# An attention and feed-forward kernel: the first product as seven block products of batch pairs

## The chip, the core and the metric

The kernel runs on one core of a Trainium2 chip. A core has TensorE (PE) for matmuls, with its weight loads shown apart as PEld; VectorE (DVE), ScalarE (ACT) and GpSimd (POOL) for element-wise work; and SyncE (SP), which here issues every DMA. The metric is the device time of one execution in microseconds.

## The reference, cut to what matters

```python
q, k, v: (8, 12, 448, 64)          # batch, heads, sequence, head size
q_n, k_n = rmsnorm(q, g_q), rmsnorm(k, g_k)
scores = matmul(q_n, k_n^T) / 8
attn = softmax(scores)             # with the maximum taken off, sum + 1e-9
x = matmul(attn, v)                # brought to (8 * 448, 768)
h = x @ w_in                       # (3584, 768) @ (768, 2048)
g = h * cos(h)
out = g @ w_out                    # (3584, 2048) @ (2048, 768)
```

w_in and w_out come as float64. Inside the kernel they are decoded from their integer halves into float32.

## The kernel before

Two heads of one batch form a pair; 48 pairs (u), six to a batch, run one after the other. Work on a pair: square sums and norms of q and k; seven score tiles S (`score`); their row minima on DVE (`rowmin`; the scores are negated) and exponentials P on ACT (`expo`); then per chunk of keys (kc, four of them) seven transposes of P into the tile PT (`transp`), copies of PT to SBUF (`pt_high`, `pt_low`), and the product P v into O. The sums' reciprocals take a way through DRAM (`rs_copy`, `rs_store`, `rs_load`) and scale O to x, with features in the partitions.

There are two ways to multiply here. Plain float32 operands go into one matmul, which the trace records as two. Split operands are a high part in fp32r (tile names with `hi`) and a low part, the rest (`lo`); three fp32r matmuls, hi hi, hi lo and lo hi, then make one product. Pairs in `S32` have plain scores, pairs in `A32` plain P v; before, both are the pairs 0 to 8. In a pair of `A32` P v is `av_whole` (L522): per chunk one matmul for each of the two heads, side by side in the halves of O. In the others it is `av` (L514): seven fp32r matmuls for each head with split P and split v, for which ACT makes `hi` (L494), DVE `lo` (L502, L504), POOL splits v (L409, L413), and x is put together from two halves (L540, L545, L548).

The first product, h = x w_in, runs per batch b as soon as its six pairs are there: 16 column blocks fc of w_in, each 18 matmuls (6 chunks of features by 3 parts, L573 to L575) into a bank `ph`, copied on ACT (`h_out`, L585) and stored to the DRAM tensor `h_d`. All split columns of w_in stay in SBUF. The first product of a batch is mixed into the attention of the next batch; that of the last batch stands alone behind the attention.

The second product, out = g w_out, already works on pairs of batches with seven block products in place of eight (the scheme of Strassen and Winograd, halving features, rows and batches): seven forms of w_out, made while attention runs and kept in the DRAM tensor `wo_d`, are streamed in through SBUF slots (`v_place`), 7 x 8 x 9 matmuls of each of three banks for a batch pair (L648 to L650).

What sets the order is the class `Plan`. Every piece of work is added with an engine, a cost, a due time, the keys it reads and writes, and for DMAs a landing time. `Plan.order` simulates the engines with these costs, takes on a free engine the ready piece that is due first, and so fixes each engine's order, which then stands in the program. Buffers are rings (`RING`): a piece waits for the user that many instances earlier. There is one plan for attention and the mixed first product and one for the rest. The pace of the pairs in the first plan is set by `base(u)`.

Of the kernel before, what the change touches and what calls it, by code (L numbers as in the profile page):

```python
# [3 lines left out]

# [23 lines left out]
class Plan:  # L28
# [40 lines left out]
    def order(self):  # L69
        parts = self.parts  # L70
        for (name, inst), users in self.users.items():
            parts[users[0]][5].update(self.users.get((name, inst - self.rings[name]), ()))
            parts[users[0]][5].update(self.users.get((name, inst - 1), ())[:1])
# [17 lines left out]
        while True:  # L91
# [21 lines left out]
            for m in after[n]:  # L113
                same = parts[m][0] == e and not land
# [12 lines left out]
def tile_attention_moe(  # L127
# [19 lines left out]
    S32, A32 = tuple(range(9)), tuple(range(9))  # L147
# [12 lines left out]
    epool = ctx.enter_context(tc.tile_pool(name="epool", bufs=2))  # L160
# [11 lines left out]
    wo_d = dpool.tile([NH, NPR, 128, 2, HM], F32, tag="wo_d", name="wo_d")  # L172
# [16 lines left out]
    def g_fold():  # L189
# [5 lines left out]
    wts, wfl, raw = {}, {}, {}  # L195
    RING = {
        "sd": 1, "r": 5, "rkb": 1, "rqb": 1, "kd": 1, "kl": 2, "khi": 2, "qd": 1, "ql": 2, "qhi": 2, "vd": 1, "vs": 2, "S": 3, "sm": 3, "P": 12,
        "hi": 4, "lo": 2, "O": 1, "xf": 6, "rs": 1, "rt": 1, "ph": 1, "he": 2, "wf": 2,
        "wx": 5, "wv": 2,
    }  # L200

    def w_load(fc):
        if f64:
            st = raw[fc] = wpool.tile([128, 2 * DM], I32, tag=f"w{fc}", name=f"raw{fc}")
            nc.sync.dma_start(st, w_in[fc].bitcast(I32))
        else:
            wfl[fc] = apool.tile([128, DM], F32, tag="wf", name=f"wf{fc}", bufs=RING["wf"])
            nc.sync.dma_start(wfl[fc], w_in[fc])
# [38 lines left out]
    def v_fetch(k, m):  # L247
        fc, cs = k + NH * (m // 2), slice(m % 2 * HM, m % 2 * HM + HM)
        f = mix[(k, m)] = apool.tile([128, HM], F32, tag="wx", name=f"wx{k}_{m}", bufs=RING["wx"])
        if f64:  # L250
            st = half[(k, m)] = apool.tile([128, DM], I32, tag="wf", name=f"rawo{k}_{m}", bufs=RING["wf"])
            nc.sync.dma_start(st, w_out[fc][:, cs].bitcast(I32))
        else:
            nc.sync.dma_start(f, w_out[fc][:, cs])

    def v_decode(k, m, step):
        decode(half[(k, m)], mix[(k, m)], step)

    def v_mix(k, to, a, c, op):
        if to == SS and (k, SS) not in mix:  # L260
            mix[(k, SS)] = apool.tile([128, HM], F32, tag="wx", name=f"wx{k}_{SS}", bufs=RING["wx"])
        nc.gpsimd.tensor_tensor(mix[(k, to)], mix[(k, a)], mix[(k, c)], op)
# [3 lines left out]
    def v_split(k, p, m, lo):  # L266
        if not lo:
            t = vts[(k, p)] = apool.tile([128, 2, HM], F32R, tag="wv", name=f"wv{k}_{p}", bufs=RING["wv"])
            nc.scalar.copy(t[:, 0, :], mix[(k, m)])
# [4 lines left out]
    def v_store(k, p):  # L274
        nc.sync.dma_start(wo_d[k, ORDER.index(p)], vts.pop((k, p)).bitcast(F32))
# [787 lines left out]
```

## Time and profile before

| | us |
|---|---|
| median of 3 runs | 1442.18 (1441.9 to 1447.97) |
| the profiled execution, as run | 1444.56 |
| its span, first to last instruction | 1442.7 |
| batch 0's first product begins | 89 |
| pair 12 done with x | 231.2 |
| attention's last x | 953.7 |
| last batch's first product alone | 959.5 to 1017.7 |
| second product and end | 1017.7 to 1442.7 |

The times within the execution are from the start of its span. The page lists for every engine its busy time; the groups list instructions of one line and shape with their mean duration; the windows give per stretch each engine's busy time and, in brackets with an x, how many instructions began there. PE's durations overlap from one matmul to the next, so counts per stretch tell more of PE than busy time.

### The profile page before, as it was taken

Reading aid. Unit: us, or ns where it says so; the run is one execution under the profiler, and the core shown is the slowest. Engines: PE = TensorE matmul, PEld = TensorE weight load, DVE = VectorE, ACT = ScalarE, POOL = GpSimd, SP = SyncE. Lnnn points to the kernel's source line nnn. Section 1 sums busy time; section 2 is a strip of 40 time slices with the busy share of each in tenths; the row PEclk is TensorE's granted clock in tenths of the full one; section 3 lists DMA queues with packets and bytes.
Section 4 is the critical chain, followed back from the end, with each engine's and each line's share of the span. In section 5 each row is a group of like instructions: output and inputs, shape, how many; then the busy total and the mean of one; then the engine's idle time right before and its main releaser. Section 6 shows DMA issues by size and latency. Waiting matters only on the chain.

```text
span 1442.7 us, 22453 instructions
## 1 busy us (share of the span) xinstructions
PE 1398.2 (97%) x7361; PEld 1154.5 (80%) x7361; DVE 1022.5 (71%) x1649; ACT 1000.2 (69%) x2058; POOL 931.0 (65%) x722
## 2 busy tenths in 40 slices
PE   6999999999999999999999999999999999999998
PEld 2445688887888888788788888889899899899897
DVE  7778986677778686878767555437876967867921
ACT  5776677667777877777776676547776786776741
POOL 5667867666887968787675663101386585676673
PEclk9999999999999999999999999999999999999999
DMA  6787444565667566666556432149579489389372
GB/s 207 216 265 230 154 125 144 157 169 182 208 201 230 190 197 217 190 208 202 180 169 188 163 123 85 47 138 354 190 238 344 137 262 338 125 295 325 114 229 100
DMA packets 154453, 282.63 MB, mean 196 GB/s; under 512 B 31760, under 2 KB 102368, under 8 KB 154336
## 3 DMA queue, kind: packets, MB, share of 16 engines
q1 hardware_dynamic: 154336, 281.20, 61.2%
q8 instruction: 58, 0.95, 0.3%
q14 instruction: 59, 0.48, 0.1%
HBM read 218.24 MB, written 62.89 MB: 195 GB/s over the span
## 4 chain that ended last, share of the span: by engine, by line
PE 67%; DVE 13%; ACT 6%; DMA 5%; issue 4%; POOL 4%; SPq 0%; ACTq 0%; DVEq 0%; POOLq 0%
PE ph L573 8%; PE PT L483 8%; PE ph L574 8%; PE ph L575 8%; PE O L514 7%; PE S L438 7%; PE y L649 7%; PE y L650 6%; PE y L648 6%; DMA hb<-h_d 3%; DVE lo L502 2%; ACT hi L494 2%; POOL glo L633 1%; PE O L522 1%; DVE sm L447 1%
## 5 line engine op out<-in xcount | busy, mean ns | idle before, releaser
L573 PE MATMUL ph<-xs,wi 128*128 128x448 f32 x768 | 298.6, 389 | 1.7 <-ACT he L585 1.6
L574 PE MATMUL ph<-xs,wi 128*128 128x448 f32 x768 | 281.2, 366 | 0.0
L575 PE MATMUL ph<-xs,wi 128*128 128x448 f32 x768 | 281.1, 366 | 0.0
L456 ACT ACTIVATE P<-S,sm 128x448 f32<-128x448 f32 x336 | 213.3, 639 | 87.5 <-DVE sm L447 73.5
L649 PE MATMUL y<-glo,wo 128*128 128x448 f32 x672 | 247.3, 368 | 6.0 <-POOL glo L633 6.0
L650 PE MATMUL y<-ghi,wo 128*128 128x448 f32 x672 | 246.8, 367 | 0.0
L648 PE MATMUL y<-ghi,wo 128*128 128x448 f32 x672 | 246.8, 367 | 0.0
L494 ACT CAST hi<-PT 128x448 fp32r<-128x448 f32 x312 | 153.2, 536 | 70.8 <-PE PT L483 35.7
L447 DVE TENSOR_REDUCE sm<-S 128x1 f32<-128x448 f32 x322 | 187.5, 612 | 15.8 <-PE S L438 15.0
L483 PEld LDWEIGHTS PT<-ident,P 128*128 128x128 f32 x1344 | 155.5, 141 | 49.1 <-issue 25.2
L502 DVE TENSOR_TENSOR lo<-PT,hi 128x448 fp32r<-128x448 f32 x234 | 135.1, 617 | 82.9 <-ACT hi L494 79.0
L483 PE MATMUL PT<-ident,P 128*128 128x128 f32 x1344 | 185.8, 276 | 2.7 <-DVE hi L492 1.3
L573 PEld LDWEIGHTS ph<-xs,wi 128*128 128x128 f32 x768 | 144.6, 188 | 32.5 <-issue 13.2
L575 PEld LDWEIGHTS ph<-xs,wi 128*128 128x128 f32 x768 | 144.4, 188 | 12.5
L574 PEld LDWEIGHTS ph<-xs,wi 128*128 128x128 f32 x768 | 145.0, 189 | 9.9 <-issue 0.6
L649 PEld LDWEIGHTS y<-glo,wo 128*128 128x128 f32 x672 | 126.6, 188 | 18.5 <-POOL glo L633 7.5
L648 PEld LDWEIGHTS y<-ghi,wo 128*128 128x128 f32 x672 | 126.6, 188 | 11.4
L650 PEld LDWEIGHTS y<-ghi,wo 128*128 128x128 f32 x672 | 126.6, 188 | 11.2
L306 POOL TENSOR_TENSOR r<-r,nhalf 128x14 f32<-128x14 f32 (+1 forms) x50 | 127.6, 2553 | 12.3 <-DVE r L324 8.5
L438 PE MATMUL S<-khi,qhi 64*128 64x448 f32 x399 | 117.9, 521 | 7.6 <-ACT P L456 4.4
L514 PE MATMUL O<-hi,vs 128*128 128x448 f32 x312 | 105.0, 386 | 2.9 <-DVE hi L504 0.9
L377 POOL TENSOR_TENSOR kl<-kd,khi 128x448 fp32r<-128x448 f32 x39 | 49.0, 1255 | 80.7 <-ACT khi L373 66.4
(225 smaller groups left out, 2755.2 us busy)
## 6 DMA issues: line engine op xcount, KB each, us to landing
wo<-wo_d SPq DMA_DIRECT2D x88, 768.0 KB
h_d<-he SPq DMA_DIRECT2D x128, 224.0 KB
hb<-h_d SPq DMA_DIRECT2D x64, 448.0 KB
wo_d<-wv SPq DMA_DIRECT2D x56, 384.0 KB
sd<-sd SPq DMA_DIRECT2D x46, 448.0 KB
vd<-v SPq DMA_DIRECT2D x78, 160.0 KB
qd<-qT SPq DMA_DIRECT2D x48, 256.0 KB
raw<-w_in SPq DMA_DIRECT2D x16, 768.0 KB
```

Source lines behind the costliest of these rows:

```text
L438: nc.tensor.matmul(d["S", t][:, :S], d[a][p0:p1, j * 128 : j * 128 + 128], d[c][p0:p1, :], start=(n == 0), stop=(n == len(ops) - 1),)
L447: nc.vector.tensor_reduce(least, d["S", t][:, :S], axis=AX.X, op=ALU.min)
L456: nc.scalar.activation(tl(u, f"P{t}", [128, S], F32, "P"), d.pop(("S", t))[:, :S], AF.Exp, bias=sm[:, 1, t : t + 1], scale=-1.0, accum_out ...
L483: nc.tensor.transpose(pt[:, t * 128 : t * 128 + 128], src, ident)
L494: nc.scalar.copy(hi, pt[:, hh * S : hh * S + S])
L514: nc.tensor.matmul(O, st, d.pop((what, kb, hh)), start=(kc + n == 0), stop=(kc + n == 4))
L573: nc.tensor.matmul(ph[:, :S], whi, x2[:, 0, :], start=(cc == 0), stop=False)
L574: nc.tensor.matmul(ph[:, :S], whi, x2[:, 1, :], start=False, stop=False)
L575: nc.tensor.matmul(ph[:, :S], wlo, x2[:, 0, :], start=False, stop=(cc == NCC - 1))
L648: nc.tensor.matmul(y, whi, hi, start=(k == 0 and chain < 2), stop=False, skip_group_check=chain == 2)
L649: nc.tensor.matmul(y, whi, lo, start=False, stop=False, skip_group_check=chain == 2)
L650: nc.tensor.matmul(y, wlo, hi, start=False, stop=(k == NH - 1), skip_group_check=chain == 2)
```

## The change

1. **The first product in seven block products.** It now takes pairs of batches. x of two batches is cut into four blocks: features 0 to 383 and 384 to 767 of the first batch, and the same of the second (a, c and b, d in `operands`). Seven operands, a, c, d and four sums or differences made by `x_mix` on DVE, are split into high and low parts (`x_split`) in the tile `opw`. For every ft (8 of them, one column block in each half of w_in's columns) there are seven block products of 9 matmuls (`ffn1`, L601 to L603 of the changed kernel: three feature chunks by three parts). Some go on in a bank that has been read in between. ACT copies a bank to a tile of `hew` (`h_copy`, L606) or DVE adds it to one (`h_add`, L609); four results per ft go to `h_d`.
2. **Forms of w_in in DRAM.** Seven split forms for each ft are made as for w_out (decode on DVE and ACT, sums and low parts on POOL, high parts on ACT), stored to `wc_d[0]`, and streamed back chunk by chunk (`c_load`, 384 KB, a ring of 8) for each batch pair anew. The two pure forms are made early (`weights_pure`), the five mixed ones later, for which two halves are kept as float32 in `wf_d`.
3. **Where it stands.** Of the first batch pair, two products (`EARLY`, of batch 0 alone) run during batch 1, and the other five (`LATE`) during batches 2 and 3, with one partial result kept in the DRAM tensor `e_d`; the pairs of batches 2, 3 and 4, 5 run during the next two batches' attention, and that of 6, 7 behind the attention.
4. **P v in plain float32 for all 48 pairs** (`A32`), plain scores for pairs 0 to 11 (`S32`). O takes one bank instead of two, and the first product gets two banks in the first plan instead of one.
5. Pace: `base` 12.5 us for each of the first 12 pairs, then 19.2; ring of P 14 instead of 12. In `Plan.order`, a DMA issue that only follows an earlier issue of the same ring no longer waits for that one's landing in the simulation.

```diff
-    S32, A32 = tuple(range(9)), tuple(range(9))
+    S32, A32 = tuple(range(12)), tuple(range(48))
...
+    FULL = ((1, 1, 0, COPY, 0, 0), (5, 0, 1, COPY, 1, 0), (3, 1, 1, COPY, 2, 0), (0, 1, 0, ADD, 2, 2),
+            (2, 0, 0, ADD, 1, 1), (4, 0, 0, ADD, 0, 0), (6, 0, 1, COPY, 3, 0))
+    EARLY = ((0, 1, 0, KEEP, 0, 0), (3, 0, 1, COPY, 1, 0))
+    LATE = ((1, 1, 0, ADD, 1, 0), (5, 0, 1, ADD, 2, 0), (2, 1, 0, ADD, 2, 2), (4, 0, 0, ADD, 1, 1), (6, 0, 1, ADD, 0, 0))
+    GROUPS = [(0, EARLY), (0, LATE)] + [(bp, FULL) for bp in range(1, B // 2)]
+    def walk(steps):
+        stride = 1 if steps is EARLY else 2
+        return sorted((len(steps) * ft + stride * i, ft, i) for ft in range(NH) for i in range(len(steps)))
...
+    def ffn1(n, pi, first, pspool, tag):
+        w = chunk(n)
+        for t in range(NT):
+            whi, wlo = (w[:, x, t * 128 : t * 128 + 128] for x in range(2))
+            hi, lo = (opw[:, pi, t, x] for x in range(2))
+            nc.tensor.matmul(y, whi, hi, start=(t == 0 and first == 1), stop=False, skip_group_check=first == 0)
+            nc.tensor.matmul(y, whi, lo, start=False, stop=False, skip_group_check=first == 0)
+            nc.tensor.matmul(y, wlo, hi, start=False, stop=(t == NT - 1), skip_group_check=first == 0)
+    def h_copy(i, tag, last):
+        nc.scalar.copy(hew[:, i % NHE], (y1.pop(tag) if last else y1[tag])[:, :S])
+    def h_add(i, a, tag, last):
+        nc.vector.tensor_tensor(hew[:, i % NHE], (y1.pop(tag) if last else y1[tag])[:, :S], hew[:, a % NHE], ALU.add)
...
+    def c_load(n):
+        nc.sync.dma_start(chunk(n).bitcast(F32), wc_d[0][CH[n][1], CH[n][2]])
...
-    BASE, PER0, PER1, PER = 12.0, 16.0, 19.0, 19.0
+    BASE, PER0, PER = 12.0, 12.5, 19.2
...
-            d["O"] = ps_o.tile([128, 2, 512], F32, tag="O", name=f"O{u}")
+            d["O"] = ps_o.tile([128, 1, 512], F32, tag="O", name=f"O{u}")
...
-                same = parts[m][0] == e and not land
+                same = parts[m][0] == e and (not land or (n, m) in self.issue)
```

The order of the instructions shows three places. First PE, at one chunk of P v in the steady part of attention. Before, after the last matmul of a block of the first product (L575), two heads with their high and low parts of P stand as four matmuls:

```order
L575 MATMUL ph_7_6373<-xs,wi_1350 128x448
L514 MATMUL O_6347<-hi_1_0_6370,vs_6029 128x448
L514 MATMUL O_6347<-lo_1_0_6391,vs_6029 128x448
L514 MATMUL O_6347<-hi_1_1_6383,vs_6029 128x448
L514 MATMUL O_6347<-lo_1_1_6404,vs_6029 128x448
L483 MATMUL PT<-ident,P_6043 128x128
```

Now, behind a block of nine (L601 to L603, operand `opw`, chunk in `wcb`), there are two, one for each head, from a plain copy of PT:

```order
L601 MATMUL h_0_6390<-opw,wcb 128x448
L602 MATMUL h_0_6390<-opw,wcb 128x448
L603 MATMUL h_0_6390<-opw,wcb 128x448
L541 MATMUL O_6629<-hi_0_0_6602,vs_6369 64x448
L541 MATMUL O_6629<-hi_0_1_6616,vs_6369 64x448
L502 MATMUL PT<-ident,P_6349 128x128
```

The low parts are gone from PE, and a matmul fills half of O's partitions. Second, DVE at about pair 10. Before, it makes low parts of P (L502) and half sums of x (L545) between the row minima (L447):

```order
L447 TENSOR_REDUCE sm_2199<-S_4_2201 128x1
L545 TENSOR_TENSOR xf_2208<-O_2036,xf_2208 64x448
L502 TENSOR_TENSOR lo_0_0_2254<-PT,hi_0_0_2236 128x448
L502 TENSOR_TENSOR lo_0_1_2259<-PT,hi_0_1_2241 128x448
L394 SCALAR_TENSOR_TENSOR ql_2278<-qd_1946,gs,qhi_2269 128x512
L469 COPY rt_2304<-PT 7x128
L502 TENSOR_TENSOR lo_1_0_2308<-PT,hi_1_0_2293 128x448
```

Now decoding of two half tiles of w_in (L228 to L236, `raw` to `wx`) stands there, one copy of PT per chunk (L511), and x in one piece (L550):

```order
L511 COPY hi_0_1_1989<-PT 128x448
L228 TENSOR_SCALAR wx_1_3_1912<-raw_1_3_1913 128x384
L230 SCALAR_TENSOR_TENSOR wx_1_3_1912<-raw_1_3_1913,wx_1_3_1912 128x384
L236 SCALAR_TENSOR_TENSOR wx_1_1_1906<-raw_1_1_1907,wx_1_1_1906 128x384
L232 SCALAR_TENSOR_TENSOR wx_1_3_1912<-raw_1_3_1913,wx_1_3_1912 128x384
L550 TENSOR_TENSOR xfw<-O_1825,rs_1916 128x448
L488 COPY rt_2039<-PT 7x128
L466 TENSOR_REDUCE sm_1886<-S_6_1954 128x1
```

Third, PE behind the attention. Before, a column block of 18 matmuls is followed by the next in another bank, and its first matmul waits for ACT alone:

```order
L573 MATMUL ph_9_11708<-xs,wi_1548 128x448
L574 MATMUL ph_9_11708<-xs,wi_1548 128x448
L575 MATMUL ph_9_11708<-xs,wi_1548 128x448
L573 MATMUL ph_10_11744<-xs,wi_1594 128x448 [waits Activation_49]
L574 MATMUL ph_10_11744<-xs,wi_1594 128x448
```

Now every ninth matmul begins a block that waits for a chunk's DMA (the DMAHW semaphore) and for the reader of its bank, here DVE, with one block of another bank (h_3) between:

```order
L601 MATMUL h_3_10712<-opw,wcb 128x448
L602 MATMUL h_3_10712<-opw,wcb 128x448
L603 MATMUL h_3_10712<-opw,wcb 128x448
L601 MATMUL h_0_10626<-opw,wcb 128x448 [waits DMAHW3_49,DVE_49]
L602 MATMUL h_0_10626<-opw,wcb 128x448
```

So the resident weights' place is taken by a stream, and one wait in 18 matmuls by two in nine.

More of the change, by code (lines that the diff above doesn't have):

```diff
@@ L39, in __init__ @@
         self.rings = rings
+        self.issue = set()
         self.parts = []
@@ L250, in v_fetch @@
         if f64:
-            st = half[(k, m)] = apool.tile([128, DM], I32, tag="wf", name=f"rawo{k}_{m}", bufs=RING["wf"])
-            nc.sync.dma_start(st, w_out[fc][:, cs].bitcast(I32))
-        else:
[L254 to L262, printed above, removed]
+            st = half[(z, k, m)] = apool.tile([128, DM], I32, tag="wf", name=f"raw{z}_{k}_{m}", bufs=RING["wf"])
@@ L416, in place @@
     def place(u, n):
-        i = 7 * min(u, NP) + (n if u < NP else 0)
-        if u < NP:
-            return ("ph", i // 4) if i % 4 == 3 else ("S", 3 * (i // 4) + i % 4)
-        return ("S", i - i // 4 + 7 * (u - NP) + n)
-    NSP = 7 * NP // 4
+        i = 7 * u + n
+        if u < 2 * NP:
+            n, i = divmod(i, NSB + 1)
+            return ("S", NSB * n + i) if i < NSB else ("ph", n)
+        return ("S", i - NSP)
+    NSP = sum(place(u, n)[0] == "ph" for u in range(2 * NP) for n in range(7))
     def score(u, j):
@@ L713, in weights2 @@
[L713 to L727 removed]
+    mixes, splits, raws = count(), count(), count()
@@ L728, in weights2, with fetch, forms @@
+    def fetch(z, k, m, key, d):
+        st = ("wf", next(raws))
+        add(SP, ISS, d - 20.0, v_fetch, z, k, m, w=[st, key] if f64 else [key], land=LAND, start=d - 30.0)
+        if f64:
+            for step, eng, cost in ((0, DVE, 0.42), (1, DVE, 0.7), (2, DVE, 0.7), (3, ACT, 0.56), (4, DVE, 0.66)):
+                add(eng, cost, d + step, v_decode, z, k, m, step,
+                    r=[st] if step != 3 else [], w=[key] if step != 3 else [st])
+    def forms(z, k, x, todo, d, gap):
         for n, (p, m, ab) in enumerate(todo):
-            e = d + n * span / 14.0
+            e = d + n * gap
@@ new lines, in weights @@
+    def weights(z, k, d0, span):
+        x = {}
+        for n, m in enumerate((X1, X2, Y1, Y2) if z else (X1, Y1, X2, Y2)):
+            x[m] = ("wx", next(mixes))
+            if z == 0 and m in (X1, Y1):
+                add(SP, ISS, d0 - 8.0, f_load, k, m, r=[("wfd", k, m)], w=[x[m]], land=LAND)
+            else:
+                fetch(z, k, m, x[m], d0 + n * span / 8.0)
+        x[SS] = ("wx", next(mixes))
+        todo = (PURE if z else ()) + MIXED
+        forms(z, k, x, todo, d0 + span / 2.0, span / (2.0 * len(todo)))
@@ L853, in attend, with keys_x @@
             add(POOL, 1.22, D2 + 5, x_norm, u, r=[("rs", u)], w=x)
[L854 to L868 removed]
+    def keys_x(u):
+        return [("X", u % (2 * NP), hh) for hh in range(2)]
```

378 lines of the change are left out of this document (210 added, 168 removed).

## The prediction

> **What bounds the kernel now.** I read the page's busy shares first, then the stages in windows, then the groups by line, then the timeline for the true price of a matmul.
>
> ```profile
> span 1442.7 us, 22453 instructions
> PE 1398.2 (97%) x7361; PEld 1154.5 (80%) x7361; DVE 1022.5 (71%) x1649; ACT 1000.2 (69%) x2058; POOL 931.0 (65%) x722
> PEld 2445688887888888788788888889899899899897
> ```
>
> PE is busy 97% of the span, so PE seems to set the time throughout. The weight loads beside it say otherwise for the start: their busy share is two to five tenths in the first four slices (36 us each). The stages show it better. I cut where pair 6, 12, 24, 36 and 48 leave attention (last write of x), at the end of the mixed part, and at the first matmul of the second product; per engine a row has busy us and instructions, and it ends with clock, DMA share and GB/s.
>
> ```profile
> 0.00:114.50 114.50, 93.95 (x413) 43.56 (x413) 87.41 (x154) 77.89 (x179) 71.46 (x57) 0.99 0.76 229
> 114.50:231.20 116.70, 113.47 (x610) 83.00 (x610) 98.82 (x142) 85.84 (x186) 92.19 (x75) 0.99 0.55 166
> 231.20:475.80 244.60, 241.62 (x1358) 199.31 (x1357) 182.54 (x307) 177.96 (x416) 179.46 (x168) 1.00 0.62 184
> 475.80:717.30 241.50, 237.92 (x1340) 196.32 (x1339) 182.95 (x310) 178.77 (x421) 187.06 (x177) 1.00 0.64 202
> 717.30:953.70 236.40, 233.01 (x1321) 194.59 (x1320) 143.85 (x254) 153.04 (x368) 112.37 (x114) 1.00 0.38 125
> 1017.70:1442.70 425.00, 414.89 (x2018) 379.40 (x2016) 289.10 (x426) 283.70 (x421) 278.64 (x125) 1.00 0.67 222
> ```
>
> The first stage issues 413 matmuls in 114.5 us, the third 1358 in 244.6: 3.6 against 5.6 a microsecond, at the same granted clock. So PE has room up to pair 12, and none from there on. The Trainium skill ("Trainium Kernel Development and Optimization", section Performance Expectations) calls matmul busy time a bad metric, because matmuls are pipelined, and points to the weight loads' share. By the PE row alone the part up to 231.2 us could lose at most 231.2 − 207.4 = 24 us; by the PEld row over 100. The counts above side with the page.
>
> **The price of a matmul.** The groups give 366 to 389 ns each, but those spans overlap.
>
> ```profile
> 1080.00:1120.00 40.00, 40.00 (x200) 1.00 0.97 336
> 210.82 0.45 PE L573 MATMUL ph<-xs,wi 128*128 128x448 f32 x1
> ...
> 214.55 0.36 PE L514 MATMUL O<-hi,vs 128*128 128x448 f32 x1
> ...
> 215.36 0.92 PE L483 MATMUL PT<-ident,P 128*128 128x128 f32 x7
> ```
>
> In the second product 200 matmuls fill 40 us (first row): 0.200 us. Between 210.82 and 214.55, amid attention, 18 first-product matmuls take 3.73 us: 0.207. The four P v matmuls from 214.55 to 215.36 take 0.81: 0.2025.
>
> **First product.** Before, 8 x 16 x 18 = 2304 matmuls; after, 4 x 7 x 8 x 9 = 2016. Where they stand counts more than the sum.
>
> ```profile
> 0.00:231.20 231.20, 34.16 (x84) 16.08 (x84) 0.99 0.66 197
> 231.20:959.50 728.30, 229.53 (x589) 110.72 (x589) 1.00 0.55 170
> 959.50:1017.70 58.20, 34.93 (x96) 17.84 (x95) 1.00 0.92 325
> ```
>
> These are L573, one of three equal lines: 252 matmuls up to 231.2, 1767 up to 959.5, and 288 alone in 58.2 us (0.202 each). After the change 144 stand ahead of pair 12's x (two of the seven products of the first batch pair), 1368 after it, and 504, a whole batch pair, behind the attention. Mixed part: 1767 − 1368 = 399 fewer, at 0.207: **−82.6 us**. Pure part: 504 x 0.202 = 101.8; the order also shows the last four blocks of nine on one bank, so three reads of it uncovered, some 0.7 us each by the copy's 0.53 us (row below) and a signal: 104 − 58.2 = **+45.6**.
>
> **P v in float32.** Each pair's 14 split matmuls (2.84 us at 0.2025) become 8 float32 ones, whose two heads run side by side.
>
> ```profile
> 46.78 1.72 PE L522 MATMUL O<-hi,vs 128*64 128x448 f32 x8
> 48.43 0.99 PE L483 MATMUL PT<-ident,P 128*128 128x128 f32 x7
> ...
> 51.05 0.97 PE L522 MATMUL O<-hi,vs 128*64 128x448 f32 x4
> 51.96 0.98 PE L483 MATMUL PT<-ident,P 128*128 128x128 f32 x7
> L514 PEld LDWEIGHTS O<-lo,vs 128*128 128x128 f32 x234 | 44.0, 188 | 17.5 <-DVE lo L502 14.4
> L585 ACT COPY he<-ph 128x448 f32<-128x448 f32 x128 | 68.1, 532 | 43.5 <-PE ph L575 34.3 <-issue 7.5 <-DMA h_d<-he 1.1
> ```
>
> Two key chunks back to back take 1.65 us (46.78 to 48.43), one alone 0.91: 3.3 to 3.64 a pair. That is 0.46 to 0.8 more; I take 0.6, times the 36 pairs from pair 12 on: **+21.6** (16 to 29). So this half costs PE time. It gives back waits: PE's loads waited 14.4 us for `lo`, which no longer exists, but the plain copies have to be waited for too. I take **−6**, ends 0 and −20.
>
> **DVE up to pair 12.** Freed of `lo` and the halves of x, DVE takes on decoding of half tiles and the mixing of x. Up to pair 12's x the changed order has on DVE:
>
> ```profile
> L447 DVE TENSOR_REDUCE sm<-S 128x1 f32<-128x448 f32 x322 | 187.5, 612 | 15.8 <-PE S L438 15.0
> L216 DVE TENSOR_SCALAR wx<-rawo 128x384 int32<-128x384 int32 x32 | 22.2, 694 | 2.9 <-DMA rawo<-w_out 2.9
> L218 DVE SCALAR_TENSOR_TENSOR wx<-rawo,wx 128x384 int32<-128x384 int32 x32 | 26.8, 839 | 0.7
> L220 DVE SCALAR_TENSOR_TENSOR wx<-rawo,wx 128x384 int32<-128x384 int32 x32 | 25.4, 795 | 0.8
> L224 DVE SCALAR_TENSOR_TENSOR wx<-rawo,wx 128x384 f32<-128x384 f32 x32 | 20.6, 650 | 1.3 <-ACT rawo L222 1.3
> L298 DVE TENSOR_REDUCE r<-sd 128x14 f32<-128x896 f32 x46 | 49.5, 1075 | 6.0 <-ACT sd L295 6.0
> L492 DVE COPY hi<-PT 128x448 f32<-128x448 f32 x27 | 16.6, 614 | 8.3 <-ACT hi L494 8.2
> L532 DVE TENSOR_TENSOR xf<-O,rs 128x448 f32<-128x448 f32 x9 | 5.5, 613 | 0.0
> ```
>
> 22 decodes at 0.69 + 0.84 + 0.80 + 0.65 = 2.98 make 65; 93 row minima at 187.5 / 322 = 0.58 make 54 (55 with the first two pairs' dearer form); 16 square sums 17; 37 copies 23; 12 x 7; 8 mixes 5, at the price of the last row; some 45 small ones 15, my estimate from their likes. Sum 187 us. Before, DVE had 87.4 + 98.8 = 186 in 231.2 us, 0.81 of the time, of which 0.85 in the second part. Its work up to pair 12 is thus not smaller. But before, PE was nearly full in that second part (113.5 of 116.7 us) with 252 matmuls of the first product; now there are 108 fewer, and DVE can run closer together. Over 120 to 200 us it did 73.1 of 80 us.
>
> ```profile
> 120.00:160.00 40.00, 37.51 (x47) 1.00 0.69 209
> 160.00:200.00 40.00, 35.59 (x55) 1.00 0.41 126
> ```
>
> That is 0.91. I take 0.88: 187 / 0.88 = 212 us, **−19**. Ends: 0.94 (the first of these rows), 199 us; 0.81, 231 us.
>
> Pairs 12 to 23 hold as much DVE work again (84 minima, 15 decodes, 39 adds of the product's blocks, 35 copies; 187 us by the same rows). PE's side: twelve pairs of attention cost 244.6 − 593 x 0.207 = 122 us before (593 being the even share of the 1767), 129 with the dearer P v; with the 39 and 51 blocks of nine that the order puts into pairs 12 to 23 and 24 to 35, PE needs 202 and 224. DVE at 0.9 takes 208 in the first of these: some +8. Pairs 24 to 35 carry the most DMA: counted from the order, 56 loads of weight chunks (22.0 MB), 38 stores of forms (14.9), 23 loads of w_out (9.0), 30.6 for attention and h, 76.5 MB in 224 us, 342 GB/s. The trace had 336 at a share of 0.97 with PE full (1080 to 1120). I charge +6. The two are **+14**, ends 0 and +35. The Trainium skill ("DMA: Bandwidth & Descriptors", section Specifications) puts a core's HBM limit at about 358 GB/s; by that, those pairs need 214 us, less than PE's 224, and this charge would be near 0. No run before shows such a rate over 200 us.
>
> The second product is the same 2016 matmuls; its operands of the first batch pair have 102 instead of 58 us ahead of them: 0.
>
> **Sum.** −19 − 82.6 + 21.6 − 6 + 14 + 45.6 = −26.4, span 1442.7 → 1416.3. The profiled execution took 1444.56, 1.9 over its span and 2.4 over the median of 1442.18, so about 1416.
>
> **Rivals.**
> *PE sets all of it.* Stage one at 199 us (−13), no charge for DVE and DMA (−14), all of the waits for `lo` gone (−14): 1375; with half of it 1395. For it: PE was full at a DMA share of 0.97. Against: DVE would need 374 / 401 = 0.93 over 400 us. Chance 0.19, 1375 to 1402.
>
> *DMA fills pairs 24 to 35.* Attention's mix made 202 GB/s at 0.64, 316 at a full share: 76.5 MB take 242 us, +18 against the +6 charged: 1428. Chance 0.13.
>
> *DVE sets the first half, no denser than before.* At 0.81 its 187 + 187 us up to pair 24 take 231 + 231 instead of 212 + 208: +42, **1458, slower**. The place is the DVE queue, where decodes, minima and adds stand in one order and each waits for its own DMA, PE or ACT. It decides at 374 / (420 + 26) = 0.84, where nothing is gained. For it: 0.81 up to 231 us, 0.75 after. Against: there PE was the full one. Slower 0.09; near 0.84 (no change) 0.10.
>
> *Hand-offs in the pure part.* 48 times PE goes on in a bank that ACT or DVE has just read, with one block (1.8 us) between; all uncovered, at 0.7, +34: 1450, but only with ACT and DVE far behind. 0.03.
>
> *That the change does not do what it says* the order excludes: 2016 first-product rows, 384 of `av_whole`.
>
> **How the numbers follow.** The forecast, 1402 to 1434, gets 0.46. With a measurable bound of 0.5% (1435 to 1449): faster 0.46 + 0.19 + 0.11 of the DMA case = 0.76; within 0.10 + 0.02 of DMA + 0.02 of the hand-offs = 0.14; slower 0.10. The range leaves out the lower part of the PE case (about 0.08) and the slower ones (0.10): 1386 to 1446.
>
> **What would show it.** Pair 12's x near 212 us with DVE at 0.88 up to there; pair 24's near 420; 504 matmuls in 104 us; P v blocks of 0.83 to 0.91; DMA near 340 GB/s in pairs 24 to 35 with few waits of PE for weight chunks (`wcb`, `wca`). I am wrong if DVE stays at 0.81 there, if PE waits for chunks, or if PE's waits on `he` copies and adds fill the pure part.

## The result and the profile after

| | time, us | ratio to before (95% interval) |
|---|---|---|
| before | 1444.12, median of 4 (1441.9 to 1447.97) | |
| changed | 1548.1, median of 4 (1546.01 to 1550.96) | 1.0719 (1.0688 to 1.075) |

The change makes the kernel 7.2% slower, 104 us, where 26 fewer were forecast. The times of the runs are medians of fast executions; one execution of e1_pv below (2271.52 us at a granted clock of 0.56) was slow and does not count. The page of the changed kernel, its first lines, the granted clock in 40 slices and the traffic (282.63 MB before):

```profile
span 1546.8 us, 22393 instructions
PE 1427.0 (92%) x7130; PEld 1047.9 (68%) x7130; DVE 997.9 (65%) x1632; ACT 925.2 (60%) x1936; POOL 869.0 (56%) x620
PEclk9989999999998999999999999879999999999999
...
DMA packets 198374, 402.70 MB, mean 260 GB/s; under 512 B 36640, under 2 KB 103408, under 8 KB 198256
```

Every engine is busy for a smaller share than before: PE 92% for 97%, DVE 65% for 71%. PE's busy time even grew, with 231 fewer matmuls in the records. Plain P v, dearer by 0.65 us a pair (below), is a part of that; another is the mean granted clock, first of before, then of the changed kernel:

```profile
core 0: 1442.7 us, clock 0.996
```

```profile
core 0: 1546.8 us, clock 0.970
```

At half clock a matmul takes nearly twice its time (in the timeline below two records of P v take 0.97 us before a stop and 1.75 after it). 3.0% of 1546.8 us is 46 us of lost clock, against 6 before; it is an upper bound, since some of it passes while PE has nothing to do. The stages, cut at the x of pairs 6, 12, 24, 36 and 48 and at the first matmul of the second product (columns as in the prediction):

```profile
0.00:132.00 132.00, 99.40 (x420) 46.23 (x420) 96.72 (x193) 84.15 (x205) 74.21 (x64) 0.94 0.87 268
132.00:237.10 105.10, 95.51 (x489) 56.06 (x490) 70.65 (x118) 72.79 (x176) 71.62 (x60) 0.98 0.94 308
237.10:489.60 252.50, 225.69 (x1148) 142.99 (x1147) 172.95 (x296) 145.31 (x351) 173.46 (x146) 0.95 0.85 271
489.60:742.00 252.40, 236.37 (x1236) 155.69 (x1235) 172.53 (x289) 154.06 (x369) 160.02 (x135) 0.97 0.90 294
742.00:981.10 239.10, 233.53 (x1276) 160.22 (x1275) 129.29 (x222) 127.12 (x317) 82.24 (x70) 0.99 0.68 217
981.10:1123.90 142.80, 123.61 (x554) 109.09 (x553) 91.03 (x140) 81.05 (x138) 29.93 (x22) 0.90 0.88 311
1123.90:1546.80 422.90, 412.95 (x2017) 377.59 (x2015) 264.68 (x378) 260.72 (x385) 277.53 (x125) 1.00 0.67 227
```

Up to 742 us no engine is busy all the time: in pairs 12 to 23 (third row) DVE is busy for 173 of 252.5 us, PE for 226 with part of that at half clock. The chain of waits, of before and of the changed kernel, by engine:

```profile
PE 67%; DVE 13%; ACT 6%; DMA 5%; issue 4%; POOL 4%; SPq 0%; ACTq 0%; DVEq 0%; POOLq 0%
```

```profile
PE 58%; DMA 17%; DVE 13%; issue 5%; POOL 4%; ACT 3%; SPq 1%; DVEq 0%; ACTq 0%; POOLq 0%
```

DMA went from 5% to 17% of the chain: work stood and waited for transfers. The two largest sums of PE's waits up to 742 us (us, times, longest), and two of DVE's:

```profile
PE O L541 <- DVE hi L511: 18.5, 14, 4.5
PE PT L502 <- DVE hi L511: 16.7, 6, 5.4
```

```profile
DVE wx L228 <- DMA raw<-w_in: 33.9, 12, 5.3
DVE wx L228 <- DMA raw<-w_out: 28.8, 11, 5.4
```

PE's list names no load of w_in or w_out, and none of a weight chunk either; it names copies of PT. The timeline joins the two lists at one place, PE first and then DVE:

```profile
307.44 0.97 PE L541 MATMUL O<-hi,vs 128*64 128x448 f32 x2
312.94 1.75 PE L541 MATMUL O<-hi,vs 128*64 128x448 f32 x2 [4.53 <-DVE hi L511]
```

```profile
309.00 0.36 DVE L228 TENSOR_SCALAR wx<-raw 128x384 int32<-128x384 int32 x1 [5.33 <-DMA raw<-w_in]
309.40 0.56 DVE L230 SCALAR_TENSOR_TENSOR wx<-raw,wx 128x384 int32<-128x384 int32 x1
...
311.80 0.55 DVE L232 SCALAR_TENSOR_TENSOR wx<-raw,wx 128x384 int32<-128x384 int32 x1
312.27 0.62 DVE L511 COPY hi<-PT 128x448 f32<-128x448 f32 x1
```

A decode stands at the head of DVE's order and waits 5.33 us for a half tile of w_in. The copy of PT that PE needs stands behind it, and behind the decode's own 3.3 us of instructions. PE stops for 4.53 us. Of the next three views, the first shows what follows (PE, PEld, DVE, ACT, POOL, clock, DMA share, GB/s), the second the issue of the half tile on SyncE, and the third the DMA rows of 285 to 320 us in 40 slices, in which it was loaded:

```profile
312.00:318.00 6.00, 4.63 (x12) 2.75 (x13) 5.45 (x9) 3.48 (x8) 3.91 (x4) 0.50 0.50 145
```

```profile
302.66 1.43 SPq L249 DMA_DIRECT2D raw<-w_in  x2
```

```profile
DMA  8759589976999999999999999999999986004445
GB/s 321 237 178 351 158 236 332 158 263 197 365 404 294 263 350 327 373 386 390 400 395 252 283 289 251 332 379 263 357 276 330 248 240 203 0 0 152 151 163 193
```

The transfer engines are at 0.9 or more for 22 slices of 0.875 us on end, and two slices later idle. A mean share of 0.85 hides such stretches of 19 us. The half tile was issued amid this one and used 6.3 us later, where the plan reckons 5; but DVE had come to the decode 1 us after the issue. So the load came late both by its issue and by its transfer, and this place does not say by which more. And once PE has stopped, its clock is 0.50 for the six microseconds after. The Trainium skill ("TensorE: Matmul & The Clock Gate", section Part 1: The HAM clock gate) describes just this: the clock is full or half, and falls after PE has been idle for a window of some 3.4 us; this trace agrees, with 0.50 after a stop of 4.53 us.

### The profile page after: what moved, and what is told of

Its sections match the earlier page's. It is cut to its first block, busy times and chain, and to the rows that moved or that the text cites. A ratio compares the mean times of both kernels' runs of the same rounds, so it can differ in the third digit from the quotient of the medians.

```text
span 1546.8 us, 22393 instructions
## 1 busy us (share of the span) xinstructions
PE 1427.0 (92%) x7130; PEld 1047.9 (68%) x7130; DVE 997.9 (65%) x1632; ACT 925.2 (60%) x1936; POOL 869.0 (56%) x620
## 4 chain that ended last, share of the span: by engine, by line
PE 58%; DMA 17%; DVE 13%; issue 5%; POOL 4%; ACT 3%; SPq 1%; DVEq 0%; ACTq 0%; POOLq 0%
PE h L601 8%; PE O L541 7%; PE PT L502 7%; PE h L602 7%; PE h L603 7%; PE S L457 6%; PE y L713 5%; PE y L714 5%; PE y L712 5%; DMA hb<-h_d 3%; DMA sd<-sd 2%; DMA raw<-w_in 2%; DMA wcb<-wc_d 2%; DVE xfw L568 2%; DMA raw<-w_out 2%
## 5 line engine op out<-in xcount | busy, mean ns | idle before, releaser
L541 PE MATMUL O<-hi,vs 128*64 128x448 f32 (+1 forms) x768 | 218.7, 580 | 43.8 <-DVE hi L511 20.0
L502 PEld LDWEIGHTS PT<-ident,P 128*128 128x128 f32 x1344 | 149.3, 144 | 153.3 <-issue 124.4
L601 PE MATMUL h<-opw,wcb 128*128 128x448 f32 x504 | 198.6, 394 | 17.5 <-DVE hew L609 10.9
L502 PE MATMUL PT<-ident,P 128*128 128x128 f32 x1344 | 196.5, 287 | 17.6 <-DVE hi L511 16.7
L513 ACT COPY hi<-PT 128x448 f32<-128x448 f32 x240 | 123.2, 534 | 145.7 <-PE PT L502 98.7
L713 PE MATMUL y<-glo,opw 128*128 128x448 f32 x540 | 198.4, 367 | 5.7 <-POOL glo L697 5.7
L712 PE MATMUL y<-ghi,opw 128*128 128x448 f32 x540 | 197.5, 366 | 0.0
L714 PE MATMUL y<-ghi,opw 128*128 128x448 f32 x540 | 197.5, 366 | 0.0
L602 PE MATMUL h<-opw,wcb 128*128 128x448 f32 x504 | 187.6, 372 | 0.0
L603 PE MATMUL h<-opw,wcb 128*128 128x448 f32 x504 | 187.5, 372 | 0.0
L575 POOL TENSOR_TENSOR opw<-xfw,opw 128x448 fp32r<-128x448 f32 x84 | 108.1, 1308 | 76.4 <-ACT opw L573 69.7
L276 POOL TENSOR_TENSOR wv<-wx,wv 128x384 fp32r<-128x384 f32 x104 | 110.4, 1070 | 45.0 <-ACT wv L273 36.1
L601 PEld LDWEIGHTS h<-opw,wcb 128*128 128x128 f32 x504 | 96.8, 192 | 54.3 <-DVE hew L609 14.8
L511 DVE COPY hi<-PT 128x448 f32<-128x448 f32 x144 | 88.4, 614 | 63.0 <-ACT hi L513 62.8
L713 PEld LDWEIGHTS y<-glo,opw 128*128 128x128 f32 x540 | 101.4, 188 | 16.9 <-POOL glo L697 8.5
L714 PEld LDWEIGHTS y<-ghi,opw 128*128 128x128 f32 x540 | 101.4, 188 | 8.4
L712 PEld LDWEIGHTS y<-ghi,opw 128*128 128x128 f32 x540 | 101.4, 188 | 8.4
```

The lines of the kernel that those rows point to most:

```text
L502: nc.tensor.transpose(pt[:, t * 128 : t * 128 + 128], src, ident)
L541: nc.tensor.matmul(d["O"][64 * hh : 64 * hh + 64, 0, :S], d["vs"][:rows, 0, hh * NVC + c], d.pop(("hi", kc, hh))[:rows], start=(kc == 0), ...
L601: nc.tensor.matmul(y, whi, hi, start=(t == 0 and first == 1), stop=False, skip_group_check=first == 0)
L602: nc.tensor.matmul(y, whi, lo, start=False, stop=False, skip_group_check=first == 0)
L603: nc.tensor.matmul(y, wlo, hi, start=False, stop=(t == NT - 1), skip_group_check=first == 0)
L712: nc.tensor.matmul(y, whi, hi, start=(k == 0 and chain < 2), stop=False, skip_group_check=chain == 2)
```

## The experiments

Before stood at 1444.1 to 1447.9 us in every comparison, so medians are set against 1548.1 us; those of e1 and e15, which edit the kernel before, against the before beside them.

| run | edit | us | ratio (95% interval) |
|---|---|---|---|
| e1_pv | before, P v all float32 | 1461.8 | 1.0106 (1.0079 to 1.0134) |
| e2_nostream | no chunk loads after the 8th | 1502.47 | 1.0376 (1.0344 to 1.0408) |
| e3_oneform | one block's forms, planned so | 1467.79 | 1.0138 (1.0112 to 1.0164) |
| e4_lastsplit | last low halves on DVE | 1550.48 | 1.0734 (1.0695 to 1.0774) |
| e5_splitpv | P v split, one bank | 1612.37 | 1.1156 (1.1106 to 1.1206) |
| e6_fewbytes | w_in loaded twice only | 1535.11 | 1.0619 (1.057 to 1.0669) |
| e7_onestep | decode of w_in in one step | 1539.83 | 1.0663 (1.0622 to 1.0704) |
| e8_landing | later landing times | 1520.12 | 1.0524 (1.0482 to 1.0565) |
| e9_nostore | no stores of forms | 1539.48 | 1.065 (1.0594 to 1.0707) |
| e10_nopool | no POOL work on forms | 1549.55 | 1.0706 (1.0651 to 1.0761) |
| e11_nodma | e2, e6 and e9 together | 1480.77 | 1.0237 (1.0188 to 1.0286) |
| e12_landing2 | e8, later behind attention too | 1541.2 | 1.0654 (1.0606 to 1.0702) |
| e13_sameorder | e3's cut in the changed order | 1489.88 | 1.0309 (1.0282 to 1.0336) |
| e14_allgone | e13 and e2 together | 1468.37 | 1.0162 (1.014 to 1.0184) |
| e15_landbefore | before, e8's landing times | 1492.62 | 1.0329 (1.0306 to 1.0351) |
| e16_hland | h's blocks land at 10 us | 1589.95 | 1.0987 (1.0945 to 1.1028) |
| e17_parts | blocks in three pieces | 1534.98 | 1.0621 (1.0575 to 1.0667) |
| e18_landparts | e17 and e8 together | 1530.03 | 1.0587 (1.0536 to 1.0638) |

**P v alone.** In the kernel before:

```diff
-    S32, A32 = tuple(range(9)), tuple(range(9))
+    S32, A32 = tuple(range(9)), tuple(range(48))
```

> The kernel before with float32 P v for all 48 pairs, nothing else (39 pairs change over). Theory 1, the price of P v on PE was taken too low: in pairs 36 to 47 of the changed kernel, at full clock, transposes and P v together cost 91.8 us against 78.0 before, 1.15 a pair; 39 x 1.15 = +45, 1489 us. The prediction's own terms (0.6 a pair, less some 6 for the waits for lo that go) give +17, 1461. Theory 2, the loss lies in the streams and the forms and not here: within 5 us of 1444.

It took 1461.8 us, 15 more than before beside it (11 to 19 by the interval): the prediction's +17, not theory 1's +45. Pairs 36 to 47 of this run, in one window:

```profile
722.80:965.60 242.80, 242.80 (x1345) 170.39 (x1342) 97.03 (x176) 124.03 (x304) 66.33 (x59) 1.00 0.36 119
```

PE is full at full clock, and the stage is 6.4 us longer than the 236.4 of before with 7 fewer first-product matmuls in it (counted in the two traces): 6.4 + 7 x 0.207 over 12 pairs is 0.65 a pair, where the prediction took 0.6.

**The product with P v split again.** In the changed kernel:

```diff
-    S32, A32 = tuple(range(12)), tuple(range(48))
+    S32, A32 = tuple(range(9)), tuple(range(9))
...
-    NSB, NHB = 3, 2
+    NSB, NHB = 3, 1
...
```

> The changed kernel with P v split again from pair 9 on, as before; P v then needs two banks for its result, so the first product gets one bank in attention instead of two, and its blocks go one output after the other there; 12 buffers of P instead of 14. The answer to the run before from the other side. Theory 1 (P v costs 1.15 a pair on PE): 1548 - 45 = 1503. The prediction's term: 1548 - 17 = 1531. Theory 2 (streams and forms): 1540 to 1555. The single bank can cost up to 56 x 0.7 us in 12 pairs where nothing lies between two blocks; if the run is slower than 1555 that is the reason and the run says nothing on P v.

1612.37 us is beyond the bound named there, so it says nothing on P v. The edit itself shows that the two parts of the change belong together: two banks for O leave the product one. What of the 64 us is the bank the run does not separate.

**The stream.**

```diff
     def c_load(n):
+        if n >= NWC:
+            return
```

> The changed kernel without the loads of the first product's weight chunks from the ninth on; the chunks' buffers keep what the first eight loads brought, so the first product's values are wrong, its work is the same. 85 MB of 403 MB of traffic go. Theory 2a, the stream fills the DMA engines in pairs 12 to 35 and makes other transfers late: pairs 12 to 35 fall from 505 us to some 475 (PE's own need at the price that pairs 36 to 47 show), total 1548 - 30 = 1518, with fewer half-clock stretches of PE. Theory 2b, the forms' preparation does it and not the stream: within 6 us of 1548. Theory 1 alone: the same as 2b.

46 us went, more than theory 2a asked. In the profiled execution 27 of them lie in pairs 12 to 23 (252.5 to 225.6), 10 in pairs 24 to 35, and 3 each up to pair 12 and behind pair 48. Pairs 36 to 47 stayed at 239.1.

**The forms of w_in.** Made for one row block, and planned so:

```diff
-    for k in range(NH):
+    for k in range(1):
...
-    for k in range(NH):
+    for k in range(1):
...
-        nc.sync.dma_start(chunk(n).bitcast(F32), wc_d[0][CH[n][1], CH[n][2]])
+        nc.sync.dma_start(chunk(n).bitcast(F32), wc_d[0][0, CH[n][2]])
```

> The changed kernel with the seven forms made for the first of the eight row blocks only; every chunk load reads that block's forms, so the stream is as large but w_in is read, decoded, mixed and stored for one block in eight. Theory 2b, the preparation holds the engines' queues up to pair 24 (19 + 14.8 us of decode waits for w_in, and what stands behind them): pair 12's x at some 205 instead of 237, pairs 12 to 23 some 15 shorter, total 1548 - 47 = 1500. Theory 2a (the stream): no more than 10 us, 1538. Theory 1 alone: within 5 of 1548 beyond pair 24, and pair 12's x unchanged.

80 us went, though the stream stayed: 21 up to pair 12, 37 in pairs 12 to 23, 22 in pairs 24 to 35. Theory 2a does not allow that; theory 2b asked for less. The forms were then taken apart in the changed kernel's own order, loads, decode, stores and POOL each alone (`half` keeps two loaded half tiles):

```diff
+            if not z and len(half) >= RING["wf"]:
+                half[(z, k, m)] = list(half.values())[len(half) % RING["wf"]]
+                return
```

> The changed kernel in which w_in is loaded for the first two half tiles only; the other 30 decodes run on those two tiles, so DVE, ACT and POOL do all of their work, the stores and the stream stay, and 11.8 MB of loads and every wait of a decode for w_in go; the first product's values are wrong. Making one block's forms instead of eight took 80 us off. Theory P, late w_in: a decode that waits for its load at the head of DVE's queue holds the copies and minima behind it (33.9 us of such waits): -35 to -50, about 1505. Theory Q, the work itself on the queues (DVE above all): 0 to -12, about 1540.

```diff
-        decode(half[(z, k, m)], mix[(z, k, m)], step)
+        if z or step == 0:
+            decode(half[(z, k, m)], mix[(z, k, m)], step)
```

> The changed kernel in which a decode of w_in is one of its five instructions, the first; 32 x (0.84 + 0.80 + 0.65) = 73 us of DVE and 18 of ACT go, every load, store and POOL instruction stays, and the values are wrong. Theory Q, DVE's work sets the time up to pair 24, as the prediction's terms have it: -40 to -60, about 1500, with pair 12's x near 212. Theory P, late loads at the head of the queues: 0 to -15, about 1540.

```diff
     def v_store(z, k, p):
+        if not z and k:
+            vts.pop((z, k, p))
+            return
...
```

> The changed kernel without the stores of the forms of w_in for seven of the eight row blocks (49 stores, 19.3 MB); every chunk load reads the first block's forms, all other work and traffic stay, the values are wrong. One block's forms alone took 80 us off, of which w_in's loads are 13 and four fifths of the decodes 8 by the runs before; some 59 are open. Theory D, traffic: the stores hold up what queues behind them, -20 to -40, 1518. Theory E, the engines' work on the forms (POOL's above all): 0 to -8, 1543.

```diff
     def v_mix(z, k, to, a, c, op):
+        if not z and k:
+            return
...
     def v_split(z, k, p, m, lo):
+        if not z and k:
+            if lo:
+                return
+            m = X2 if m == SS else m
...
```

> The changed kernel without POOL's part in the forms of w_in for seven of the eight row blocks: 28 mixes and 49 low halves, 77 x 1.1 = some 85 us of POOL; the stores write the high half twice, so the traffic stays. The values are wrong. Theory E, POOL's queue is where the time goes (decoded tiles, the pairs' norms and low halves stand in one order there): -30 to -50, 1508. Theory D, traffic: 0 to -8, 1543.

They gave 13, 8, 9 and nothing (+1). So neither late w_in (theory P) nor DVE's work (theory Q) is the cause by itself, nor are stores or POOL. e6_fewbytes removes the very wait seen in the timeline. Up to 742 us of it, one of DVE's and one of PE's waits:

```profile
DVE wx L228 <- DMA raw<-w_in: 2.4, 1, 2.4
```

```profile
PE h L604 <- DVE hew L612: 11.0, 4, 7.2
```

The decodes' waits for w_in fell from 33.9 us to 2.4, and PE's for DVE's copies of PT from 35.2 to 14.7. But other waits of PE grew, those for block results (here L604 on L612) from 3.9 us to 11.0, and only 13 us came off. The decode run is as telling. Up to pair 12's x, of the changed kernel and then of that run:

```profile
0.00:237.10 237.10, 194.91 (x909) 102.29 (x910) 167.37 (x310) 156.94 (x380) 145.84 (x124) 0.96 0.90 286
```

```profile
0.00:234.50 234.50, 194.17 (x910) 101.75 (x910) 129.10 (x246) 147.22 (x358) 142.23 (x124) 0.95 0.92 289
```

38 us of DVE work left that part, and 2.6 us of time. All parts at once, in the unchanged order, the code as in the four edits, with the loads and stores of `wf_d` dropped too:

> The changed kernel in its own order, from which every instruction and transfer that makes forms of w_in for seven of the eight row blocks is dropped (loads, decodes, mixes, halves, stores); every chunk load reads the first block's forms, values wrong. The run with one block's forms left the same out but planned without them, and was 80 us faster; its parts dropped alone in the changed kernel's order gave 13, 8, 8 and 0. Theory N, the parts cover for each other (a queue that loses one wait meets the next): again -70 to -85, 1470. Theory O, a good part of the 80 is the other order that the planner makes with fewer parts: -30 to -45, 1510.

58 us went: twice the 28 of the single cuts, and 22 short of the 80. Both theories hold in part: the cuts bring more together than singly, and 22 us of e3's gain are the other order that the planner made with less to place. The 4.53 us stop above shows one way in which parts cover for each other: copy and PE waited for a load and then for the decode, so without the decode the wait for the load still stands there. How much of the 30 us over the single cuts is such covering is open, since this run also drops what no single cut dropped: the first step of the decodes, ACT's high halves and the transfers of `wf_d`.

**All traffic of w_in, then everything.** The stream, the loads and the stores of the forms dropped together:

> Three cuts at once in the changed kernel: no chunk loads after the eighth, w_in loaded for two half tiles only, no stores of forms for seven of eight blocks; 116 MB of 403 go and every engine does all of its work. The values are wrong. Theory D, traffic makes everything late up to pair 36: 1548 - 46 - 13 - 30 = 1459, near the kernel before. Theory E: no more than the two cuts already measured, 1548 - 46 - 13 = 1489, and less where they cover each other, up to 1500.

1480.77 us, 67 less, is about the sum of 46, 13 and 9: the cuts of traffic add up. Its stages up to pair 36:

```profile
0.00:118.80 118.80, 93.62 (x420) 44.34 (x420) 102.73 (x193) 84.24 (x204) 75.16 (x64) 1.00 0.71 216
118.80:220.10 101.30, 95.34 (x490) 55.89 (x490) 73.13 (x120) 72.55 (x176) 71.92 (x59) 1.00 0.67 201
220.10:440.20 220.10, 212.15 (x1150) 137.49 (x1148) 171.86 (x295) 145.38 (x350) 174.78 (x147) 0.99 0.57 172
440.20:678.50 238.30, 228.92 (x1233) 152.75 (x1233) 177.63 (x290) 153.32 (x369) 160.91 (x135) 0.99 0.70 227
```

DVE, ACT and POOL do as much as in the changed kernel, and the clock is back at 0.99 to 1.00. Then e13 without the stream:

> As the run before, without the chunk loads after the eighth too: what is left is the block products, the float32 P v and their hand-offs, in the changed kernel's order. Theory N: 1470 - 40 = 1430, some 14 under the kernel before; with PE full up to pair 48 the prediction's counts (no stream, no forms) would give 1375 to 1400. Theory O: 1470, still slower than the kernel before.

At 1468.37 us the change is still 1.6% slower than before, with no stream and with one eighth of the forms. Its stages:

```profile
0.00:114.70 114.70, 92.30 (x420) 44.47 (x420) 69.72 (x142) 74.33 (x181) 60.33 (x53) 0.99 0.66 206
114.70:211.50 96.80, 94.36 (x490) 55.88 (x490) 58.25 (x100) 66.70 (x163) 57.90 (x47) 1.00 0.67 203
211.50:424.60 213.10, 209.18 (x1150) 136.03 (x1148) 146.17 (x254) 127.96 (x311) 119.62 (x93) 1.00 0.56 169
424.60:664.20 239.60, 228.95 (x1232) 153.05 (x1232) 175.79 (x289) 153.41 (x369) 161.43 (x135) 0.99 0.69 225
664.20:903.80 239.60, 233.96 (x1275) 160.04 (x1275) 132.15 (x221) 126.91 (x316) 83.74 (x70) 0.99 0.38 125
903.80:1043.60 139.80, 121.40 (x554) 107.64 (x553) 91.01 (x141) 80.31 (x138) 29.95 (x22) 0.91 0.49 166
```

Up to pair 24 the clock is back at 0.99 to 1.00, and pair 12's x stands at 211.5 us with DVE busy for 128 of them, 0.60. The last two rows hardly moved. Against e11_nodma the engines' work on the forms and the transfers of `wf_d` are worth 12 us, so of the 80 us that went the other transfers of w_in account for 67.

**Order alone.** The planner sets each engine's order from assumed landing times of transfers. Later ones, nothing left out:

```diff
-    ISS, LAND = 0.45, 5.0
+    ISS, LAND = 0.45, 8.0
...
-        add(SP, ISS, D0 - 45, st_load, u, w=sd, land=6.5)
+        add(SP, ISS, D0 - 45, st_load, u, w=sd, land=10.0)
...
```

> The changed kernel with the planner told that transfers in attention land later: 8 us for 5, 10 for 6.5, 9 for 6, 12 for 8. Only the order of the instructions changes, nothing is left out. Theory P, instructions stand at the heads of queues before their data can be there: -20 to -40, about 1518. Theory Q, and also that DMA is simply full: within 8 us of 1548.

28 us went, as theory P asks, but not evenly: pairs 12 to 23 took 208.4 us, pairs 24 to 35 273.6, with 60 first-product matmuls moved from the first to the second. The same in the kernel before:

> The kernel before with the later landing times (8, 10, 9, 12 us) in attention that made the changed kernel 28 us faster. Theory T, the kernel before has PE full with spare traffic, so lateness costs it nothing and the order hardly matters: within 6 us of 1447. Theory U, the landing times are too short in either kernel: -10 or more, 1437 or less, and then it is the fastest of all.

It became 47 us slower, its first 12 pairs 257.2 us for 232.4. Neither theory had that, and it takes theory P's reading from the run before: the landing times are not simply too short. An order fits one kernel: the same change of the plan's numbers moved the one by −1.8% and the other by +3.3%.

**The part behind the attention.** Low halves of the last operands shared with DVE:

```diff
+        eng, cost, ns = (DVE, 0.62, nc.vector) if last and t < 2 else (POOL, 1.22, nc.gpsimd)
```

> The changed kernel with two thirds of the low halves of the last batch pair's operands on DVE (0.62 us each) instead of POOL (1.22). Between pair 48's x and the second product the changed kernel takes 142.8 us for 551 matmuls, 31 more than at 0.203 each. Theory R, the series of 21 low halves on POOL, which the mixes that overwrite x wait for, starves PE at the start of that part: -12 to -18, 1533. Theory S, the copies and sums of the product's results stand behind the second product's preparation on ACT and DVE: no more than -4, 1545.

1550.48 us: theory R falls (the part itself took 139.9 us for 142.8). What PE waits for there, in the changed kernel from 981 to 1124 us, and the place of the longest wait, on ACT:

```profile
PE h L601 <- ACT hew L606: 9.2, 4, 5.4
PE h L601 <- DVE hew L609: 5.8, 5, 1.9
```

```profile
1030.11 0.92 ACT L699 CAST ghi<-B0a 128x896 fp32r<-128x896 f32 x1
1033.62 0.55 ACT L665 ACTIVATE n0b<-hb 128x448 int32<-128x448 f32 x1 [2.58 <-DMA hb<-h_d]
1034.10 0.62 ACT L683 ACTIVATE c0a<-B0a,halfpi 128x448 f32<-128x448 f32 x1
1034.66 0.52 ACT L606 COPY hew<-h 128x448 f32<-128x448 f32 x1
```

The copy that PE waits for (5.37 us, up to 1035.24) stands behind a second-product instruction that waits for its block of h. Two attempts to plan around it, the first with this edit:

```diff
-            add(SP, ISS, d - 30.0, gl_load, pr, role, g, r=r, w=[hb], land=LAND)
+            add(SP, ISS, d - 30.0, gl_load, pr, role, g, r=r, w=[hb], land=10.0)
```

> The changed kernel with one landing time changed, that of h's blocks for the second product: 10 us for 5. In the last 504 first-product matmuls PE waits up to 5.5 us (7 to 11 in other runs) for a copy that stands on ACT behind a second-product instruction that waits for its block of h. Theory S: that wait goes and 4 to 8 us with it, 1542. If another instruction takes its place at the head of ACT: within 2 us of 1548.

> The changed kernel with the later landing times of the run before (28 us faster than the changed kernel) in the part behind the attention as well: 8 us for h's blocks, 12 for the second product's weights. Theory S, the copies and sums of the last 504 first-product matmuls stand on ACT and DVE behind second-product instructions that wait for h's blocks: -8 to -15 against that run, 1508. Theory R (the operands' splits at the start of that part) or full transfers: within 4 us of 1520.

Neither settles theory S: e16 was 42 us slower, 36 of them in the second product (458.8 us for 422.9), e12 21 us slower than e8, 22 of them there (444.5 for 422.8), while the part itself took 151.8 and 139.7 us for 142.8 and 141.2.

**The length of the blocks.** Nine matmuls planned as three pieces:

```diff
+            for ts in ((0,), (1,), (2,)) if pspool is ps_h else (range(NT),):
+                add(PE, 1.85 * len(ts) / NT, d + 0.6 * ts[0], ffn1, c, pi, first, pspool, tag, ts, r=r, w=y + e + [("done", pi)])
```

> The changed kernel with each block of nine first-product matmuls in attention planned as three pieces of three, which the planner may put apart; nothing left out. Without any forms or stream the changed kernel still takes 239.6 us for pairs 36 to 47, as with them, 13 over the prediction's 226, with PE full: transposes, P v and scores cost 12 us more there than in the kernel before with float32 P v. Theory V, the long blocks leave too few of them between the hand-offs (10 of 47 runs of transposes go straight into a block, against 43 of 48): pairs 36 to 47 fall to 226 to 231, the total by 15 to 25 with pairs 12 to 35. Theory W, the length of the blocks is not it: pairs 36 to 47 stay at 236 to 240. By itself a new order has moved the total by -28 to +42, so that stage decides and not the total.

Pairs 36 to 47 in that run:

```profile
723.20:964.70 241.50, 236.50 (x1289) 161.24 (x1288) 135.11 (x230) 133.57 (x323) 86.95 (x75) 0.98 0.69 226
```

241.5 us with 13 more matmuls of the product (2.7 us): theory W. The total fell by 13, within what an order does. With e8's landing times as well:

> The three pieces together with the later landing times in attention that took 28 us off (1520): the best that the runs so far point to. Theory V: pairs 36 to 47 from 229 to 222 or less, the total 1500 to 1510. Theory W: 1515 to 1525. Under either it stays above the kernel before (1444).

1530.03 us, 10 more than e8 alone and beyond either theory: the two do not add up. No run found a version faster than the kernel before.

## Why the prediction was wrong

Its terms give a time for each stage, and the same cuts stand beside them (us; pairs 24 to 35 as 224 + 6; pairs 36 to 47 as 236.4 less 78 matmuls at 0.207, plus 12 x 0.6, less a third of the 6; the next row holds the last 47 matmuls of the mixed part beside the pure part's 104):

| up to, or pairs | forecast | changed | e11_nodma | e14_allgone |
|---|---|---|---|---|
| pair 12's x | 212 | 237.1 | 220.1 | 211.5 |
| 12 to 23 | 208 | 252.5 | 220.1 | 213.1 |
| 24 to 35 | 230 | 252.4 | 238.3 | 239.6 |
| 36 to 47 | 226 | 239.1 | 239.1 | 239.6 |
| to the second product | 116 | 142.8 | 141.2 | 139.8 |
| second product | 425 | 422.9 | 424.8 | 424.3 |

That e14_allgone meets the 212 is chance: the forecast had 187 us of DVE work there at 0.88, that run has 128 at 0.60.

- **The step that failed: DVE at 0.88 up to pair 12 (−19) and +14 for DVE and DMA after it.** It took an engine's work over a density as the time of a stage, and put the new traffic at +6 in pairs 24 to 35 and at nothing before them.

  The density. The counts of DVE's work up to pair 12 came out (22 decodes, 16 square sums, 37 copies, 8 mixes), and count times mean duration makes some 185 us for the forecast's 187. But these durations overlap, while 0.88 was read from busy time: by busy time it is 167 us, 0.71 of the stage, and 38 us less gave 2.6 us. Even with the transfers of w_in gone DVE was busy for 0.80 of the time up to pair 12 and 0.78 in pairs 12 to 23.

  The traffic. DMA's share was 0.87 and 0.94 in the two windows up to pair 12 and 0.85 in pairs 12 to 23, where the traffic had no term; in pairs 24 to 35 it was 0.90, at 294 GB/s. The first three rows of the table lost 92 us against the forecast: 28 with nearly all transfers of w_in gone and the engines' work kept (e11_nodma), 14 with the forms' work gone too (e14_allgone). So some 64 of the 92 us are the traffic's.

  How the traffic costs time is seen in the timeline: a late transfer at the head of one in-order queue holds what others need, PE stops, and its clock halves. That all 64 us go this way is not shown; the one kind of wait that was removed alone, the decodes' for w_in, gave 13 us.
- **The clock was no term.** All durations were taken at 0.996. At 0.970 up to 46 us are lost; with traffic and forms gone 0.987. No run separates the clock from the stops before it, but the rows give an estimate for the first three stages, 742.0 us against e14_allgone's 664.2 with as many matmuls (3293 and 3292): PE is idle for 46 us more, and busy for 32 us more, which is mostly the clock (0.94 to 0.98 for 0.99 to 1.00).
- **P v in float32, +21.6 − 6:** right within the error; alone +15 (11 to 19) against the +17 of its own terms for 39 pairs.
- **Mixed part, −82.6:** the counts came out (1368 matmuls after pair 12). The price of 0.207 did not hold where PE was taken as full: pairs 36 to 47 took 239.1 us for 226. From e1's 242.8, 71 fewer matmuls at 0.207 make 228; of the 11 left, 5.6 are PE not busy (233.53 of 239.10, against all of 242.80 in e1), some 2 the clock at 0.99; the rest is open. The traffic is not it (239.6 without), nor the length of the blocks. The order may be: in e8_landing the stage took 229.1 us with 3 more first-product matmuls, but 32 fewer of attention's, half a pair's, fell in it.
- **Pure part, +45.6:** 104 forecast, 127 measured from the end of the 1512th matmul on. Nearly all of the 23 lie in its first 48 us, in waits for the block results and for the last operands, then at half clock. The last three reads on one bank were uncovered as forecast, 0.88 each for 0.7. The rival *hand-offs in the pure part* had a part of this right, at a chance of 0.03: PE did wait for results that ACT and DVE had not yet read, but the half clock that followed was no part of it.
- **Second product, 0:** right, within 2 us.
- **The rivals.** *DVE sets the first half* came nearest (1458) and on the right side, with its 231 us for each of the first two rows (237.1 and 252.5), but mostly not by its reason: with the transfers of w_in gone and DVE's work kept they took 220.1 each. *DMA fills pairs 24 to 35*: a share of 0.90, and the loss was larger in pairs 12 to 23 at 0.85. The mean rate taken for those pairs, 342 GB/s, never came (294). In the pure part 362 at a full share were seen (window below), so the Trainium skill's limit of about 358 ("DMA: Bandwidth & Descriptors", section Specifications) was reached there; by their mean, pairs 24 to 35 stayed under it.

```profile
1045.00:1120.00 75.00, 73.57 (x362) 67.48 (x361) 53.76 (x87) 44.18 (x74) 0.00 (x0) 1.00 1.00 362
```

## What to carry to other kernels

Work over a density does not give the time of a stage whose engines wait for each other. Here some of the critical engine's work was taken away and two fifths were added to the traffic, and late transfers at the heads of in-order queues then stopped that engine; so price new waits and new traffic in every stage, not only where the mean share of DMA is expected to be highest. Where PE stops for 4 or 5 us, price its matmuls of the next few microseconds at half clock (0.50 up to 318 us after the stop of 4.53 us). When several causes may cover for each other, remove them singly and together, and keep the instruction order while doing it, since a new order alone moved these kernels by 28 us down to 47 us up.

## What was not expected of the hardware

- Full transfer engines (share 1.00) moved 362 GB/s in the pure part with PE at full clock beside them, while a mean share of 0.85 in pairs 12 to 23 held 19 us of engines at 0.9 or more and idle ones right behind.
- Stops of PE brought stretches at half clock (after one of 4.53 us 0.50 from 312 to 318 us, after one of 5.36 us 0.50 from 236 to 240 us), and such stretches pulled whole stages to 0.94 to 0.98; in the kernel before no stage of attention was under 0.99.
- The cost of plain float32 P v, taken from the first nine pairs of the kernel before, held where it was measured again, in pairs 36 to 47 of e1_pv: 0.65 us a pair for 0.6.
